# Fourier mixing and GEGLU layers: z^T by VectorE and a round trip through DRAM, layer norm statistics by ScalarE

## The chip, the cores and the metric

The kernel runs on one core of a Trainium2 chip. TensorE (PE) multiplies; PEld is the loading of its stationary operand, which overlaps with it. VectorE (DVE), ScalarE (ACT) and GpSimd (POOL) work on tiles in SBUF, the first two on PSUM as well. SyncE (SP) issues loads from DRAM on one queue, POOL issues most stores on another; both use the core's 16 DMA engines. The metric is the time on the device in microseconds (us), the median of several runs.

## The reference

Four layers over x of 2048 x 512 in fp32: layers 0 and 2 are Fourier mixing, layers 1 and 3 a GEGLU feed-forward, each behind a layer norm without gains and with its input added back.

```python
def _layernorm(x, axis=-1, eps=1e-5):
    m = jnp.mean(x, axis=axis, keepdims=True)
    v = jnp.var(x, axis=axis, keepdims=True)
    return (x - m) / jnp.sqrt(v + eps)
def _A_ref(x, dft_seq_re, dft_seq_im, dft_hid_re, dft_hid_im):
    a = jnp.einsum("bsd,ed->bse", x, dft_hid_re)
    b = jnp.einsum("bsd,ed->bse", x, dft_hid_im)
    y = jnp.einsum("ts,bse->bte", dft_seq_re, a) - jnp.einsum("ts,bse->bte", dft_seq_im, b)
    return y
def _B_ref(x, w_gate, w_up, w_down):
    return (_gelu(x @ w_gate) * (x @ w_up)) @ w_down
x = x + _A_ref(_layernorm(x), ...)
x = x + _B_ref(_layernorm(x), ...)
x = x + _A_ref(_layernorm(x), ...)
x = x + _B_ref(_layernorm(x), ...)
```

The sequence matrices are 2048 x 2048, the hidden ones 512 x 512, w_gate and w_up 512 x 1792, w_down 1792 x 512. They come in as arrays, so the kernel reads them; it assumes nothing of their values.

## The kernel before, in words

*Precision.* Every fp32 operand of a product is split into a high part in fp32r (ACT, L110) and the rest (DVE, L111), and `mm3` (L142 to L146) makes one product out of three matmuls: high by high, high by low, low by high. A matmul takes 128x128 weights and 128x512 moving data.

*Fewer products.* The large products are done by one step of a Strassen-Winograd scheme on 2 x 2 blocks: seven block products instead of eight, whose operands are sums and differences of blocks (names S1 to S4 on the matrix's side, T1 to T4 on the side of the normalized input z). Sums are DVE's (`plus`, L135; `minus`, L132); copies out of PSUM are ACT's (`copied`, L139).

*Tiles.* Everything lies in slots of 128 x 512 fp32 in SBUF (`sb`, 102 of them) and eight PSUM banks (`ps8`). A slot that is freed goes to the end of a list and is taken again in that order, so a load into it waits for its last reader.

*Mixing layers (0 and 2).* `plan` runs over four blocks b of 512 rows of the sequence matrices, and within each over stages (A11, A12, S2, S3, A22 on the sequence side, then three groups of the hidden side). A stage runs over k, the 128-row tiles of z along the sequence, eight to a half. For each k, `take` hands out the next matrix tile `ws` of a list `items`: it loads ahead (four items ahead of the split, which is up to five ahead of the use: RAW = 4, AHEAD = 5) and splits ahead. The contraction is over the sequence, so here z is used as it is, rows on partitions.

*GEGLU layers (1 and 3).* Two halves w of 1024 tokens. Gate and up products are made transposed, features on partitions, so z^T is wanted: `block_steps` (L441) normalizes eight row tiles, and PE turns them with 128x128 transposes against an identity (`turned`, L450 to L457, 16 into four PSUM banks' width for each group of four tiles). From PSUM the blocks are copied, subtracted and split. `up(n)` makes the gate or up product of one pair of feature tiles in seven block products; from n = 6 on, steps of the down product (`down_steps`) are put between them; afterwards the remaining down products run one after the other, part 0 and then part 1, and `x_add` adds the input's rows and stores them (POOL's queue). The split down weights lie in DRAM as `wd`, the split and summed gate and up weights as `wb`; both are made once. `weight_steps` makes `wb` from the raw `wgu`, in layer 1 with the first half's work; `down_weight_steps` makes `wd` during layer 0.

*Layer norm.* `normed` (L368): DVE's bn_stats and bn_aggr, an addition of eps, POOL's power of -1/2, DVE's product for the shift, and ACT's scaling of the row tile (L382).

*The order.* Work that isn't on the path of products stands as closures in a list `queue`; `step` runs the next one after a product. In layers 0 and 2 a step follows each k, in the down products each item, in layer 1's first half each block product. On top of this a scheduler of the framework orders each engine's instructions by times that it reckons itself. The program orders SP's DMAs by eight semaphores in turn.

## Time and profile before

| | |
|---|---|
| median of 3 runs | 1665.11 us (1663.8 to 1665.39) |
| profiled execution | 1666.76 us, its span 1664.9 us |
| PE, PEld | 1650.4 and 1359.2 us busy (99%, 82%) |
| DVE, ACT, POOL | 1190.7, 776.2 and 169.3 us busy (72%, 47%, 10%) |
| DMA | 388.46 MB, 233 GB/s over the span |

Busy time of PE is that of pipelined matmuls whose ends are modelled, so 99% doesn't say that PE is at its peak; the chain of work that ended last tells better what sets the end. In the groups by line a row gives the line, the engine, the operation, output and inputs with their sizes, the count, busy time and mean duration, and the idle time of the engine just before with what ended it. Transposes, copies and splits all run through helpers, so their lines are those of the helpers. Layer 0 lasts to about 440 us, layer 1 to 845, layer 2 to 1210, layer 3 to the end.

### The profile page before, as it was taken

To read this page: it belongs to the slowest core of one execution; us is meant where nothing else is said; L and a number is where in the kernel's file an instruction comes from. 1 tells how busy PE (TensorE), PEld (TensorE's weight loads), DVE (VectorE), ACT (ScalarE), POOL (GpSimd) and SP (SyncE) were. 2 spreads that over 40 slices of the span, in tenths; PEclk is the share of its full clock that TensorE was granted. 3 is DMA by queue.
4 is the path that set the end of the run, shared out by engine and by line. 5 is a ranking of instruction groups with operands and counts; after the bars stand their busy time and mean duration, and the time that the engine had idled before them with its cause. 6 is when DMAs were issued, how large, how long until landed. Compare 5 with 4: busy or idle time off the path is not lost.

```text
span 1664.9 us, 22527 instructions
## 1 busy us (share of the span) xinstructions
PE 1650.4 (99%) x7296; PEld 1359.2 (82%) x7296; DVE 1190.7 (72%) x2132; ACT 776.2 (47%) x1352; POOL 169.3 (10%) x288
## 2 busy tenths in 40 slices
PE   9999999999999999999999999999999999999999
PEld 6877788888788888888888888888888888888887
DVE  8997978687887765655898785857946556656561
ACT  7744434255565543534663333444635443444440
POOL 3212100021422110000210000000100000100000
PEclk9999999999999999999999999999999999999999
DMA  9788886778766876555665766565695559755551
GB/s 361 247 279 329 306 317 227 253 252 291 273 229 215 292 269 233 172 189 198 216 227 182 240 228 228 168 227 188 225 386 184 171 177 321 259 178 175 186 183 51
DMA packets 200726, 388.46 MB, mean 233 GB/s; under 512 B 23840, under 2 KB 27424, under 8 KB 200608
## 3 DMA queue, kind: packets, MB, share of 16 engines
q1 hardware_dynamic: 183168, 329.86, 59.1%
q0 software_dynamic: 17440, 57.16, 9.1%
q8 instruction: 58, 0.95, 0.2%
q14 instruction: 60, 0.49, 0.1%
HBM read 328.73 MB, written 58.20 MB: 232 GB/s over the span
## 4 chain that ended last, share of the span: by engine, by line
PE 93%; DVE 3%; DMA 2%; issue 1%; ACT 1%; SPq 0%; DVEq 0%; ACTq 0%
PE p L144 31%; PE p L145 30%; PE p L146 30%; DMA s<-wgu 2%; DVE s L111 1%; PE p L551 1%; PE p L454 1%; DVE s L135 1%; DMA s<-ws 1%; DVE s L132 1%; DMA s<-x 0%; DVE s L725 0%; DVE s L739 0%; DVE s L723 0%; ACT s L110 0%
## 5 line engine op out<-in xcount | busy, mean ns | idle before, releaser
L145 PE MATMUL p<-s,s 128*128 128x512 f32 x2368 | 921.7, 390 | 1.9 <-DVE s L111 1.9
L146 PE MATMUL p<-s,s 128*128 128x512 f32 x2368 | 908.6, 390 | 0.0
L144 PE MATMUL p<-s,s 128*128 128x512 f32 x2368 | 901.2, 391 | 7.0 <-DVE s L135 3.9
L110 ACT ACTIVATE s<-s 128x512 fp32r<-128x512 f32 (+1 forms) x758 | 438.0, 617 | 467.6 <-DVE s L132 98.6
L111 DVE TENSOR_TENSOR s<-s,s 128x512 fp32r<-128x512 f32 (+1 forms) x758 | 490.2, 679 | 87.1 <-ACT s L110 64.3
L144 PEld LDWEIGHTS p<-s,s 128*128 128x128 f32 x2368 | 445.0, 188 | 102.9 <-DVE s L135 5.0
L145 PEld LDWEIGHTS p<-s,s 128*128 128x128 f32 x2368 | 445.4, 188 | 95.0 <-DVE s L111 3.1
L146 PEld LDWEIGHTS p<-s,s 128*128 128x128 f32 x2368 | 445.2, 188 | 93.7 <-DVE s L111 0.7
L135 DVE TENSOR_TENSOR s<-s,p 128x512 f32<-128x512 f32 x316 | 213.0, 685 | 188.9 <-PE p L146 140.6
L139 ACT ACTIVATE s<-p 128x512 f32<-128x512 f32 x248 | 145.2, 593 | 187.4 <-PE p L146 171.4
L132 DVE TENSOR_TENSOR s<-s,s 128x512 f32<-128x512 f32 (+1 forms) x290 | 172.4, 608 | 23.4 <-DMA s<-ws 15.4
L722 ACT ACTIVATE s<-s 128x512 f32<-128x512 f32 x112 | 70.4, 630 | 91.7 <-DVE s L135 90.9
L725 DVE SCALAR_TENSOR_TENSOR s<-s,s 128x512 f32<-128x512 f32 x112 | 76.8, 690 | 38.2 <-ACT s L724 37.6
L378 POOL TENSOR_TENSOR rstd<-rstd,power 128x1 f32<-128x1 f32 x64 | 50.8, 803 | 506.7 <-DVE rstd L377 500.8
L723 DVE SCALAR_TENSOR_TENSOR s<-s,s 128x512 f32<-128x512 f32 x112 | 77.0, 690 | 33.5 <-ACT s L722 31.3
L724 ACT ACTIVATE s<-s 128x512 f32<-128x512 f32 x112 | 69.5, 627 | 25.0 <-DVE s L723 24.4
L135 DVE TENSOR_TENSOR s<-s,s 128x512 f32<-128x512 f32 (+1 forms) x78 | 50.1, 645 | 38.5 <-DMA s<-ws 22.1
L169 POOL DMA_DIRECT2D x<-s x48 | 26.1, 543 | 443.8 <-DVE s L135 440.8
L382 ACT ACTIVATE s<-s,shift,rstd 128x512 f32<-128x512 f32 x64 | 50.4, 811 | 36.5 <-DVE shift L380 32.1
L739 DVE SCALAR_TENSOR_TENSOR s<-s,s 128x512 f32<-128x512 f32 x84 | 58.0, 690 | 1.6
L197 POOL DMA_DIRECT2D wb<-s x84 | 45.2, 540 | 121.6 <-ACT s L110 85.1
L373 DVE BATCH_NORM_STATS2 st<-s 128x6 f32<-128x512 f32 x64 | 42.7, 689 | 19.8 <-DMA s<-x 19.8
(32 smaller groups left out, 254.6 us busy)
## 6 DMA issues: line engine op xcount, KB each, us to landing
s<-ws SPq DMA_DIRECT2D x432, 256.0 KB, 4.0
s<-wb SPq DMA_DIRECT2D x294, 256.0 KB, 4.1
s<-wd SPq DMA_DIRECT2D x224, 256.0 KB, 4.3
s<-x SPq DMA_DIRECT2D x126, 256.0 KB, 4.1
s<-wh SPq DMA_DIRECT2D x120, 256.0 KB, 4.8
wb<-s POOLq DMA_DIRECT2D x98, 256.0 KB, 3.5
x<-s POOLq DMA_DIRECT2D x48, 256.0 KB, 4.1
wd<-s POOLq DMA_DIRECT2D x28, 256.0 KB, 4.9
```

The costliest lines, as they stand in the source:

```text
L110: nc.scalar.activation(hi, src, AF.Copy)
L111: nc.vector.tensor_tensor(lo, src, f32(hi), op=ALU.subtract)
L132: nc.vector.tensor_tensor(out, a, b, op=ALU.subtract)
L135: nc.vector.tensor_tensor(out, a, b, op=ALU.add)
L139: nc.scalar.activation(v, src, AF.Copy)
L144: nc.tensor.matmul(ps, ah, bh, start=start, stop=False, skip_group_check=True)
L145: nc.tensor.matmul(ps, ah, bl, start=False, stop=False, skip_group_check=True)
L146: nc.tensor.matmul(ps, al, bh, start=False, stop=stop, skip_group_check=True)
L722: nc.scalar.activation(t, g, AF.Square)
L723: nc.vector.scalar_tensor_tensor(t, t, 1.0 / GELU_C, g, op0=ALU.add, op1=ALU.mult)
L724: nc.scalar.activation(t, t, AF.Tanh, scale=GELU_A * GELU_C)
L725: nc.vector.scalar_tensor_tensor(t, t, 1.0, g, op0=ALU.add, op1=ALU.mult)
```

## The change: what it does

- *z^T.* Each normalized 128x512 tile is turned by DVE in 32x32 blocks into one wide tile of 128 x 2048 (one buffer); when four tiles are in it, POOL stores it (1 MB) to DRAM, and SP reads z^T back, each 128x512 tile by four DMAs of 32 partitions with runs of 128 fp32 (512 bytes). The transposes on PE and the copies out of PSUM are gone.
- *Row order.* The tokens of a 512-token group come out in another order: column tile j holds the rows 32j to 32j + 31 of each of the four row tiles. So x lies in DRAM in groups of 512 rows, and the GEGLU layers load and store it with four runs of 32 rows to a tile (`rows(..., mixed=True)`). The last four tiles of a GEGLU layer's output stay in SBUF for the next mixing layer, in that order, and `seq_tile` reads the sequence matrix's rows for k of 12 and above in four runs of 32 rows to match (layer 2 alone).
- *Statistics.* In layers 1 to 3 ACT makes the sum (Copy with an accumulator), the mean, the sum of squared deviations (Square with bias and an accumulator); POOL divides by 512, adds eps and takes the power; ACT makes the shift. Layer 0 keeps DVE's statistics. Half of layer 2's are made ahead in layer 1's second half (`terms_ahead`), from rows loaded for it.
- *Weights.* `down_weight_steps` is gone: the down weights are loaded raw, split and stored at their first use in layer 1's first half (`make_down_first`). The loads of `weight_steps` are a step of their own, issued earlier than the sums and splits.
- *Order.* The norms of layers 1 and 3 stand in the queue of block 2 (of 0 to 3) of the mixing layer ahead, instead of the last stage but one; `step` follows each block product of the up phase; items that come split from DRAM are read ahead by two beyond the use and two beyond the split (NEAR = 2). There are 98 slots instead of 102, and a pool of twelve for the early statistics.

```diff
+NEAR = 2
 EARLY = 2
 SKEW = 2
-NSLOT = 102
+NSLOT = 98
...
-    og = out.rearrange("(n p) d -> n p d", p=P)
-    xs = {(0, i): xg[i] for i in range(NS)}
+    xg = x_in.rearrange("(g r) d -> g r d", r=TB)
+    og = out.rearrange("(g r) d -> g r d", r=TB)
+    xs = {(0, g): xg[g] for g in range(NB)}
     for layer in range(1, 4):
-        for i in range(NS):
-            xs[layer, i] = dram.tile([P, D], F32, name=f"x{layer}_{i}")
-    xs.update({(4, i): og[i] for i in range(NS)})
+        for g in range(NB):
+            xs[layer, g] = dram.tile([TB, D], F32, name=f"x{layer}_{g}")
...
     fresh = {}
-    def x_load(layer, i):
+    def rows(layer, i, mixed=False):
+        g, n = divmod(i, NT)
+        if mixed:
+            return xs[layer, g].rearrange("(n j t) d -> j n t d", n=NT, t=32)[n]
+        return xs[layer, g][n * P:(n + 1) * P]
+    def x_load(layer, i, mixed=False):
         t = sb.get()
-        nc.sync.dma_start(t, xs[layer, i])
+        nc.sync.dma_start(t, rows(layer, i, mixed))
...
-    def x_add(layer, i, t, ps, keep=False, engine=nc.gpsimd):
+    def x_add(layer, i, t, ps, mixed=False, keep=False, engine=nc.gpsimd):
         plus(t, t, ps)
         ps8.put(ps)
-        engine.dma_start(xs[layer + 1, i], t)
+        engine.dma_start(rows(layer + 1, i, mixed), t)
...
     def split_next():
         n = stream["split"]
         while stream["loaded"] <= min(n + RAW, len(items) - 1):
+            if stream["loaded"] > n + NEAR and items[stream["loaded"]][2] is whole:
+                break
             load_next()
         parts[n] = items[n][2](*raws.pop(n))
...
             need = items[stream["split"]][3]
             if need and need not in cs and stream["split"] > n:
                 break
+            if items[stream["split"]][2] is whole and stream["split"] > n + NEAR:
+                break
             split_next()
...
+    def whole(*parts):
+        return parts
+    def make_down_first(f):
+        def run(v):
+            p = plain(v)
+            kept(wds[f], p)
+            return p
+        return run
...
+    def seq_tile(layer, n, k):
+        if layer and k >= NS - NT:
+            return ws[(n + 1) * NS - NT:(n + 1) * NS, (k % NT) * 32:(k % NT + 1) * 32]
+        return ws[n * NS + k]
...
-        for _ in range(NB // 2):
-            items.extend((F32R, halves(wds[f]), lambda *w: w, None) for _ in range(2) for f in range(NF))
+        for w in range(NB // 2):
+            for part in range(2):
+                for f in range(NF):
+                    if layer == w == part == 0:
+                        items.append((F32, (wdn[f],), make_down_first(f), None))
+                    else:
+                        items.append((F32R, halves(wds[f]), whole, None))
...
+    known = {}
+    def row_of(layer, i):
+        x = fresh.pop(i, None)
+        return x_load(layer, i) if x is None else x
+    def norm_terms(layer, i, x, junk):
+        pool = spool if layer == 0 else kpool
+        rstd = pool.tile([P, 1], F32, name="rstd")
+        shift = pool.tile([P, 1], F32, name="shift")
+        if layer == 0:
+            st = spool.tile([P, 6], F32, name="st")
+            nc.vector.bn_stats(st, x)
+            mv = spool.tile([P, 2], F32, name="mv")
+            nc.vector.bn_aggr(mv, st)
+            nc.vector.tensor_scalar_add(rstd, mv[:, 1:2], EPS)
+            nc.gpsimd.tensor_tensor(rstd, rstd, power, op=ALU.pow)
+            nc.vector.scalar_tensor_tensor(shift, mv[:, 0:1], -1.0, rstd, op0=ALU.mult, op1=ALU.mult)
+        else:
+            total = spool.tile([P, 1], F32, name="total")
+            mean = spool.tile([P, 1], F32, name="mean")
+            nc.scalar.activation(junk, x, AF.Copy, accum_out=total)
+            nc.scalar.activation(mean, total, AF.Copy, scale=-1.0 / D)
+            nc.scalar.activation(junk, x, AF.Square, bias=mean, accum_out=rstd)
+            nc.gpsimd.tensor_scalar(rstd, rstd, 1.0 / D, EPS, op0=ALU.mult, op1=ALU.add)
+            nc.gpsimd.tensor_tensor(rstd, rstd, power, op=ALU.pow)
+            nc.scalar.activation(shift, mean, AF.Copy, scale=rstd)
+        return rstd, shift
+    def terms_ahead(layer, i):
+        x, junk = x_load(layer, i), sb.get()
+        known[layer, i] = norm_terms(layer, i, x, junk)
+        sb.put(x, junk)
     def normed(layer, i):
-        x = fresh.pop(i, None)
-        if x is None:
-            x = x_load(layer, i)
-        st = spool.tile([P, 6], F32, name="st")
-        nc.vector.bn_stats(st, x)
-        mv = spool.tile([P, 2], F32, name="mv")
-        nc.vector.bn_aggr(mv, st)
-        rstd = spool.tile([P, 1], F32, name="rstd")
-        nc.vector.tensor_scalar_add(rstd, mv[:, 1:2], EPS)
-        nc.gpsimd.tensor_tensor(rstd, rstd, power, op=ALU.pow)
-        shift = spool.tile([P, 1], F32, name="shift")
-        nc.vector.scalar_tensor_tensor(shift, mv[:, 0:1], -1.0, rstd, op0=ALU.mult, op1=ALU.mult)
+        x = row_of(layer, i)
         z = sb.get()
...
     def block_steps(layer, w):
-        z, t = {}, {}
+        zt, t, wide = {}, {}, {}
+        turned = [dram.tile([P, NT * D], F32, name=f"t{layer}_{w}_{part}") for part in range(2)]
         def norm(i):
             def run():
-                z[i] = normed(layer, w * 2 * NT + i)
+                z = normed(layer, w * 2 * NT + i)
+                part, n = divmod(i, NT)
+                if n == 0:
+                    wide[part] = tpool.tile([P, NT * D], F32, name="wide")
+                to = wide[part].rearrange("p (b n t) -> p b n t", n=NT, t=32)
+                nc.vector.transpose(to[:, :, n], z.rearrange("p (b t) -> p b t", t=32))
+                sb.put(z)
+                if n == NT - 1:
+                    nc.gpsimd.dma_start(turned[part], wide.pop(part))
             return run
...
-            if c == ND - 1:
-                sb.put(*(z.pop(part * NT + i) for i in range(NT)))
-            return ps
+        def fetch(c):
+            def run():
+                for part in range(2):
+                    v = zt[c, part] = sb.get()
+                    for i in range(P // 32):
+                        cols = turned[part][:, (c * 4 + i) * P:(c * 4 + i + 1) * P]
+                        to = v[i * 32:(i + 1) * 32]
+                        nc.sync.dma_start(
+                            to.rearrange("p (j t) -> p j t", t=P), cols.rearrange("(j p) t -> p j t", p=32)
+                        )
+            return run
...
         def first(c):
             def run():
-                ps = turned(c, 0)
-                t[f"B{1 + c // 2}1", c % 2] = copied(ps)
-                blocks[f"B{1 + c // 2}1", c % 2] = split_slot(ps)
-                ps8.put(ps)
+                v = t[f"B{1 + c // 2}1", c % 2] = zt.pop((c, 0))
+                blocks[f"B{1 + c // 2}1", c % 2] = split_slot(v)
             return run
         def second(c):
             def run():
-                ps = turned(c, 1)
+                v = zt.pop((c, 1))
                 if c < 2:
-                    t["B12", c] = copied(ps)
-                    t["T1", c] = difference(ps, t["B11", c])
+                    t["B12", c] = v
+                    t["T1", c] = difference(v, t["B11", c])
                     sb.put(t.pop(("B11", c)))
                 else:
                     c0 = c - 2
-                    t["T2", c0] = difference(ps, t["T1", c0])
-                    t["T3", c0] = difference(ps, t["B12", c0])
+                    t["T2", c0] = difference(v, t["T1", c0])
+                    t["T3", c0] = difference(v, t["B12", c0])
                     sb.put(t.pop(("B12", c0)))
-                    blocks["B22", c0] = split_slot(ps)
-                ps8.put(ps)
+                    blocks["B22", c0] = split_slot(v)
+                    sb.put(v)
             return run
...
-        two = [norm(i) for i in range(NT, 2 * NT)] + [second(c) for c in range(ND)]
+        one = [norm(i) for i in range(2 * NT)]
+        two = [fetch(c) for c in range(ND)] + [first(c) for c in range(ND)] + [second(c) for c in range(ND)]
         two += [fourth(c) for c in range(2)]
         two += [divide(name, c) for name in ("T2", "T3", "T1", "T4") for c in range(2)]
-        return one + two
+        return one, two
...
             sides[b] = side
+            if b == NB - 2:
+                norms, others = block_steps(layer + 1, 0)
+                queue.extend([run for norm in norms[:NT] for run in (norm, None)])
+                rest.extend((norms[NT:], others))
             if last and layer == 0:
-                queue.extend(weight_steps(0))
+                opening_weights.update((n, weight_steps(n)) for n in range(2))
+                queue.extend([opening_weights[0][0], None, opening_weights[1][0], None, *opening_weights[0][1]])
             for second, k in skewed():
                 if second:
...
             if last:
-                queue.extend(block_steps(layer + 1, 0))
+                queue.extend(rest[1])
                 if layer == 0:
-                    queue.extend(weight_steps(1))
+                    queue.extend(opening_weights[1][1])
+            if b == NB - 2:
+                queue.extend([run for norm in rest[0] for run in (norm, None)])
             for second, k in skewed():
                 if second:
...
-        return [load, store]
+        return load, [sums] + [divide(i) for i in range(len(pieces))]
     def weight_load(n):
         tiles = [sb.get(F32R) for _ in range(7)]
@@ -759,14 +823,16 @@
                 yield
             sb.put(*hs, *v)
-        making = layer == 1 and w == 0
+        making = {}
+        if layer == 1 and w == 0:
+            making.update((n, weight_steps(n)) for n in range(2, NF))
+            making[2][0]()
         chain, side, c11, u, w4 = {}, {}, {}, {}, {}
         def product(n, ps, an, bn, start, stop):
-            if making:
-                step()
+            step()
             hi, lo = wparts[n][an]
             for c in range(2):
                 cut = slice(c * P, (c + 1) * P)
...
         def up(n, down):
+            if n + 3 in making:
+                making[n + 3][0]()
+            if n + 2 in making:
+                queue.extend(making[n + 2][1])
             product(n, chain[n], "S2", "T2", False, True)
             u[n] = copied(chain[n])
             next(down, None)
...
             sb.put(*wparts.pop(n)["tiles"])
-            if making and n + 3 < NF:
-                queue.extend(weight_steps(n + 3))
-            elif not making and n + 2 < NF:
+            if not making and n + 2 < NF:
                 weight_load(n + 2)
         def down(f, part):
...
-                x_add(layer, (w * 2 + 1) * NT + i, xrows.pop(0), acc[1][i], engine=nc.sync)
+                x_add(layer, (w * 2 + 1) * NT + i, xrows.pop(0), acc[1][i], True, engine=nc.sync)
...
         load_rows(0)
-        if before_mix:
+        if w == 0:
+            queue.extend(run for part in block_steps(layer, 1) for run in part)
+        elif before_mix:
             queue.extend((lambda k=k: first_rows(layer + 1, k)) for k in range(NK))
+            for k in range(NT):
+                queue.append(lambda k=k: second_rows(layer + 1, k))
+                queue.append(lambda k=k: combine(k))
+            queue.extend((lambda k=k: combine_late(k)) for k in range(NT))
         for f in range(NF - LAG, NF):
             down(f, 0)
         add_rows(0)
         if w == 0:
             weight_load(0)
             weight_load(1)
-            queue.extend(block_steps(layer, 1))
-        elif before_mix:
-            for k in range(NT):
-                queue.append(lambda k=k: second_rows(layer + 1, k))
-                queue.append(lambda k=k: combine(k))
...
         queue += [lambda k=k: combine_late(k), None]
-    for run in [run for f in range(NF) for run in down_weight_steps(f)]:
-        queue += [run, None, None]
     for layer in range(4):
```

37 lines of the change are left out of this document (12 added, 25 removed).

## The prediction

> **What bounds the kernel now.** I read the page's busy table first, then the chain that ended last, then the groups by line, then windows over single stages, then the DMA view.
>
> ```profile
> span 1664.9 us, 22527 instructions
> PE 1650.4 (99%) x7296; PEld 1359.2 (82%) x7296; DVE 1190.7 (72%) x2132; ACT 776.2 (47%) x1352; POOL 169.3 (10%) x288
> PE 93%; DVE 3%; DMA 2%; issue 1%; ACT 1%; SPq 0%; DVEq 0%; ACTq 0%
> ```
>
> TensorE is the bound: 93% of the chain lies on it. What it issues counts, then, unless a change makes it wait. From the chain in order of time and from the windows (columns: stretch, PE busy and count, PEld, DVE, ACT, POOL, clock, DMA share, GB/s):
>
> ```profile
> 889.51 0.68 PE p L144 x3
> 1195.54 1.75 PE p L454 x16
> ...
> 430.00:446.00 16.00, 13.12 (x55) 10.06 (x54) 10.32 (x21) 8.68 (x16) 4.83 (x9) 0.98 0.76 266
> 845.00:1210.00 365.00, 365.00 (x1627) 302.26 (x1626) 284.33 (x498) 169.62 (x294) 18.24 (x30) 1.00 0.65 214
> 1210.00:1560.00 350.00, 350.00 (x1561) 290.05 (x1561) 203.78 (x335) 151.09 (x261) 12.08 (x20) 1.00 0.67 228
> ```
>
> A product matmul (L144) takes 0.68/3 = 0.227 us of the chain, a transpose (L454) 1.75/16 = 0.109. From 845 to 1560 us PE is busy without a gap. Around the start of layer 1 it is not: 55 matmuls are 55 x 0.227 = 12.5 us of the 16, so 3.5 us are lost there. The stage 845 to 1210 is layer 2; its DMA share of 0.65 will matter.
>
> ```profile
> L454 PE MATMUL p<-ident,s 128*128 128x128 f32 x128 | 17.0, 272 | 0.0
> L139 ACT ACTIVATE s<-p 128x512 f32<-128x512 f32 x248 | 145.2, 593 | 187.4 <-PE p L146 171.4 <-PE p L454 10.7 <-DVE s L725 2.2
> L110 ACT ACTIVATE s<-s 128x512 fp32r<-128x512 f32 x728 | 427.3, 626 | 459.2 <-PE p L146 95.0 <-DVE s L132 90.4 <-PE p L145 65.7
> L111 DVE TENSOR_TENSOR s<-s,s 128x512 fp32r<-128x512 f32 x728 | 478.8, 690 | 85.8 <-ACT s L110 63.0 <-PE p L145 6.7 <-PE p L146 5.5
> L373 DVE BATCH_NORM_STATS2 st<-s 128x6 f32<-128x512 f32 x64 | 42.7, 689 | 19.8 <-DMA s<-x 19.8
> L375 DVE BATCH_NORM_AGGREGATE mv<-st 128x2 f32<-128x6 f32 x64 | 10.3, 176 | 0.1
> L377 DVE TENSOR_SCALAR rstd<-mv 128x1 f32<-128x1 f32 x64 | 8.2, 151 | 0.4
> L380 DVE SCALAR_TENSOR_TENSOR shift<-mv,rstd 128x1 f32<-128x1 f32 x64 | 9.9, 158 | 11.6 <-POOL rstd L378 11.1
> L378 POOL TENSOR_TENSOR rstd<-rstd,power 128x1 f32<-128x1 f32 x64 | 50.8, 803 | 506.7 <-DVE rstd L377 500.8 <-ACT s L110 2.7 <-DVE shift L380 2.2
> L80 ACT ACTIVATE warm<-warm 128x1 f32<-128x1 f32 x1 | 0.2, 204 | 0.0
> ```
>
> And the DMA view (share of 16 engines; issue to landing in us), with the waits of 845 to 1210 us:
>
> ```profile
> DMA packets 200726, 388.46 MB, mean 233 GB/s; under 512 B 23840, under 2 KB 27424, under 8 KB 200608
> q1 hardware_dynamic: 183168, 329.86, 59.1%
> s<-ws SPq DMA_DIRECT2D x432, 256.0 KB, 4.0
> s<-wd SPq DMA_DIRECT2D x224, 256.0 KB, 4.3
> ...
> s<-wgu SPq DMA_DIRECT2D x28, 128.0 KB, 3.4
> ...
> out<-s SPq DMA_DIRECT2D x4, 256.0 KB, 2.0
> ```
>
> ```profile
> ACT s L110 <- DMA s<-ws: 31.7, 16, 4.5
> ...
> DVE s L135 <- DMA s<-ws: 13.3, 7, 3.0
> DVE s L132 <- DMA s<-ws: 12.6, 14, 2.4
> ```
>
> In layer 2, ACT and DVE already wait 57.6 us for the sequence matrix's tiles, which does not reach PE because tiles are split ahead of their use.
>
> **The change part by part.** *Transposes off PE.* 128 x 0.109 = 14.0 us leave the chain. The group's mean of 272 ns is a pipelined duration, not a spacing. The Trainium skill (TensorE: Matmul & The Clock Gate, Part 4: PE-mode transpose) gives a transpose in a kernel about 275 ns; by that 35.2 us would go, 21.2 more than by the chain. The duration agrees with it, the spacing of 0.109 us does not, and it is the spacing that PE pays.
>
> *Copies and statistics.* Off ACT: 24 copies out of PSUM, 24 x 0.593 = 14.2 us. Off DVE: the statistics of 48 row tiles, 48 x (689+176+151+158 ns) = 56.4 us. Onto DVE: 32 transposes of 128x512. No row shows one; ends 0.69 us (any fp32 pass, L111) and twice that for its scattered write. I take 0.69, 22.1 us: as many elements per partition. Onto ACT: 48 x (2 x 0.626 + 2 x 0.204) = 79.7 us; onto POOL 48 more small operations, 48 x 0.803 = 38.5. An accumulating pass may take longer than 0.626; the dear end is L382's 811 ns, 0.2 us more. Net DVE falls by 34 us, ACT rises to 842, about 51%. Busy time is covered on both, but the order is not free: the shift on ACT now stands behind ACT, POOL, POOL, and whatever is queued on ACT behind it (splits that PE needs, and loads into the slots that these free) waits 2 x 0.803 = 1.6 us per tile. In layer 2's third block four tiles stand close together there. Ends 0 and 4 x 1.6 = 6.4 us; I take 3.
>
> *The way through DRAM.* Eight stores of 1 MB on POOL's queue, 128 loads of 64 KB on SP's. A 64-KB load is bounded by 2.0 us (the fastest 256-KB row) and 3.4 (the 128-KB row). SP's DMAs use eight semaphores in turn, so at most eight fly: 32 loads take at most 32/8 x 3.4 = 13.6 us, the store before them no more than four times a 256-KB landing of 4.3, 17 us. In the changed program's order, the transposed half that is latest against its use is layer 3's last: from what its last transpose needs to the first matmul that reads it stand 122 matmuls, 27.7 us. The store at half its dear end plus the loads fit, at both dear ends 3 us are missing. I take 0.
>
> *Weights.* The down weights' 14 loads of 256 KB, splits and stores leave layer 0 for their first use in layer 1, where 28 loads back fall away: 14 x (0.626 ACT, 0.690 DVE) moves, beside PE. The gate weights' loads are issued a step earlier, which meets the 3.5 us lost at 430 to 446; ends 0 and 3.5, and I take 3.5, as the loads then have a stage instead of their landing. *The shorter read-ahead* (NEAR) leaves the down weights four items of 12 matmuls, 4 x 2.7 = 10.9 us, over a landing of 4.3: nothing.
>
> *The order of rows.* The transposes leave a 512-token block in an order of 4 x 32 rows. So 32 loads of x, 32 stores of x and, in layer 2, 64 loads of the sequence matrix (all for k of 12 and above) have in DRAM an outer count of 4, not 128. A 256-KB load costs 0.262/329.86 x 0.591 x 1664.9 = 0.78 us on each of 16 engines. No row shows a load with an outer count under 128. Ends: 0.78 us as now, or, if rows are dealt by the outer count, four engines carry it alone: 3.13 us on them. I take the second: the 23840 small packets are 16 for each of the 1490 DMAs of the table (17 rows, of which the first and the last stand above), so each is closed by 16 engines with equal shares of 128 rows, and four blocks cannot be shared equally by more than four.
>
> The Trainium skill (DMA: Bandwidth & Descriptors, Rules for kernel authors) has this rule: an outermost size under 16 confines a DMA to that many engines. No trace here can show it yet.
>
> Layer 2, then: 0.65 x 365 = 237 us busy per engine now. Less 64 x 0.78 = 50, plus 64 x 3.13 = 200, plus z^T's 4 MB (two stores, eight tiles read) 12: 399 us on four engines in a stage of 365. Every 128-row load also needs those four, so all loads queue: 34 us short. Were everything a tenth cheaper, 359 us, nothing would be short. It is uneven too: in the new order, at the layer's start, six of seven loads that follow each other are such, 6 x 3.13 + 0.78 = 19.6 us, plus 2.0 landing and 1.3 for the split, and the seventh is used 64 matmuls, 14.5 us, after the first may go: 8 us late. The read-ahead of 40 to 100 matmuls (9 to 23 us, 4.0 of it the landing now) smooths some 10 us once. Layer 2 loses 34 - 10 = 24 us; ends 0 and 34 + 8 = 42. ACT's 3 us hide in it. Between the halves of layer 1, where the four x loads, 14 gate weights and z^T's 32 loads meet, 4 more (ends 0 and 14).
>
> The sum: -14.0 - 3.5 + 24 + 4 = +10.5 on the profiled execution's 1666.76 us (span 1664.9 and 1.9 around it): 1677.3. That execution stood 1.65 above the median, so 1675.6; I say 1676.
>
> **The rivals.**
> *All 16 engines carry the 4 x 32 loads.* For it: nothing in the profile shows them confined, and DMA has a third of layer 2 free. Then layer 2 keeps 3 us of ACT's waits: 1665.1 - 14.0 - 3.5 + 3 = 1651, faster; it decides once a 4 x 32 load lands in about the 4.0 us of the others. 30 in 100.
> *Four engines, but the read-ahead covers most.* DMA's price is at its low end, layer 2 loses 10, the halves nothing: 1665.1 - 17.5 + 10 = 1658 to 1662. Against it: the 57.6 us of waits for these tiles today. 12 in 100, 5 faster and 7 within 0.2%.
> *The way through DRAM is late.* The first of a half's loads waits for the store at the head of SP's in-order queue, and the down weights behind it wait too: at the store's dear end 17 us, against a read-ahead of 10.9, so 6.1 at each of four places, and the 3 us missing at the tight one: 1665.1 - 17.5 + 24.4 + 3 = 1675, slower. It decides once the queue is held for over 10.9 us. Against it: a 256-KB store lands in about the time of a load, so 17 us would need four of them one after the other. 3 in 100.
>
> **How the numbers follow.** The forecast has 55 in 100, its own range 1668 to 1700. A difference under 0.2% (3.3 us) can't be told from none here. Slower: 55 + 3 = 58; same 7; faster 30 + 5 = 35. The range must reach the first rival: 1648 to 1699, leaving out some 7 below and 8 above.
>
> **What would show it.** Right: no L454 and PE without waits at block changes; in layer 2 ACT and DVE wait for ws far beyond 57.6 us, ws landings well above 4.0, PE gaps in 845 to 1210 of some 24 us, and fewer than 16 small packets for each of these DMAs. At 430 to 446 no PE gap. Wrong: 4 x 32 loads that land like the rest, or PE full in layer 2; then the first rival holds and the time is near 1651. Much over 1700 would mean that the queue of four engines reaches layers 1 and 3 as well.

## The result, and the profile after

The changed kernel takes 1855.53 us (median; 1848.99 to 1857.9) beside 1665.25 us for the kernel before on the same chip: ratio 1.1135, 95% interval 1.1104 to 1.1167. The forecast was 1676 us, range 1648 to 1699. The direction was right, the size was not: 190 us instead of 11. The profiled execution of the changed kernel took 1857.9 us, 2.4 above its median.

From the page of the changed kernel: the span, the busy engines, TensorE's granted clock in 40 slices (tenths), the chain that ended last by engine, and the packets.

```profile
span 1856.1 us, 22573 instructions
PE 1693.9 (91%) x7168; PEld 1372.4 (74%) x7168; DVE 1168.8 (63%) x1972; ACT 839.2 (45%) x1616; POOL 193.9 (10%) x344
PEclk9999999999999889999788999989979999989999
PE 51%; issue 23%; DMA 16%; DVE 5%; ACT 3%; SPq 1%; POOL 1%; DVEq 0%; ACTq 0%; POOLq 0%
DMA packets 221607, 400.03 MB, mean 216 GB/s; under 512 B 29872, under 2 KB 49840, under 8 KB 220464
```

PE has 128 instructions fewer and is busy 43.5 us longer (1693.9 against 1650.4), at a clock that now falls in the middle of the span. The chain, 93% PE before, is 51% PE, and 16% DMA stands in it.

Windows over the stages, each from its first product matmul to the next stage's (columns as in the prediction's windows: stretch, PE busy and count, PEld, DVE, ACT, POOL, clock, DMA share, GB/s). The stages are layer 0, layer 1's two halves, layer 2, layer 3's two halves. First the kernel before, then the changed one:

```profile
7.50:414.80 407.30, 401.43 (x1745) 325.48 (x1745) 350.47 (x652) 208.76 (x364) 67.47 (x105) 1.00 0.82 287
414.80:633.70 218.90, 215.84 (x958) 177.51 (x957) 165.28 (x312) 113.53 (x206) 54.52 (x102) 0.99 0.74 259
633.70:843.10 209.40, 209.40 (x925) 173.40 (x924) 138.52 (x260) 103.11 (x178) 11.88 (x20) 1.00 0.60 195
843.10:1238.60 395.50, 395.50 (x1761) 327.50 (x1760) 299.20 (x522) 176.81 (x307) 20.21 (x34) 1.00 0.68 227
1238.60:1451.70 213.10, 213.10 (x958) 176.70 (x957) 127.45 (x217) 94.12 (x161) 9.92 (x17) 1.00 0.67 226
1451.70:1660.90 209.20, 209.20 (x925) 173.21 (x923) 106.67 (x163) 77.61 (x133) 3.57 (x7) 1.00 0.49 163
```

```profile
7.80:417.70 409.90, 402.06 (x1713) 324.84 (x1713) 344.63 (x620) 213.75 (x398) 63.78 (x99) 0.98 0.80 271
417.70:639.00 221.30, 212.09 (x925) 174.03 (x924) 153.25 (x275) 122.23 (x246) 67.32 (x126) 0.98 0.75 256
639.00:867.00 228.00, 215.28 (x926) 176.50 (x925) 129.44 (x211) 120.79 (x251) 16.22 (x32) 0.97 0.66 208
867.00:1410.00 543.00, 432.14 (x1730) 342.95 (x1729) 308.38 (x503) 198.34 (x383) 26.71 (x48) 0.88 0.57 175
1410.00:1621.60 211.60, 209.78 (x926) 173.10 (x924) 109.01 (x169) 96.46 (x190) 12.53 (x25) 1.00 0.66 215
1621.60:1846.80 225.20, 215.86 (x923) 174.93 (x924) 120.84 (x187) 85.29 (x146) 5.57 (x8) 0.97 0.59 184
```

So layer 0 ends at 415 us, layer 1 at 843 and layer 2 at 1239, and not at 440, 845 and 1210 as said ahead of the prediction. Layer 2 alone lost 147.5 us of the 191.2 between the spans, and the second halves of layers 1 and 3 another 18.6 and 16.0; 5.3 us more lie behind the last matmul (1856.1 - 1846.8 against 1664.9 - 1660.9), where the last stores are. Note the DMA share of layer 2: it fell from 0.68 to 0.57. The stage became longer than its transfers; the sixteen engines as a whole were never the limit. The waits of layer 2 (867 to 1410) say for whom it waited:

```profile
ACT s L113 <- DMA s<-ws: 112.2, 31, 9.7
...
DVE s L138 <- DMA s<-ws: 51.3, 15, 7.4
...
DVE s L135 <- DMA s<-ws: 38.8, 18, 4.0
```

202 us for the tiles of the sequence matrix, against 57.6 before, and now they reach PE, which waits 35.4 us there for ACT's splits and 34.4 for DVE's.

### The profile page after: what moved, and what is told of

It reads as the page before. It is cut to its first block, busy times and chain, and to the rows that moved or that the text cites. A ratio compares the mean times of both kernels' runs of the same rounds, so it can differ in the third digit from the quotient of the medians.

```text
span 1856.1 us, 22573 instructions
## 1 busy us (share of the span) xinstructions
PE 1693.9 (91%) x7168; PEld 1372.4 (74%) x7168; DVE 1168.8 (63%) x1972; ACT 839.2 (45%) x1616; POOL 193.9 (10%) x344
## 2 busy tenths in 40 slices
DMA packets 221607, 400.03 MB, mean 216 GB/s; under 512 B 29872, under 2 KB 49840, under 8 KB 220464
## 4 chain that ended last, share of the span: by engine, by line
PE 51%; issue 23%; DMA 16%; DVE 5%; ACT 3%; SPq 1%; POOL 1%; DVEq 0%; ACTq 0%; POOLq 0%
PE p L148 17%; PE p L147 17%; PE p L149 17%; DMA s<-ws 6%; DMA s<-x 4%; DVE s L114 2%; DVE s L135 2%; DMA x<-s 1%; DMA s<-wb 1%; DMA s<-wh 1%; ACT s L113 1%; DVE s L138 1%; DMA s<-wd 1%; PE p L624 1%; DMA s<-wgu 1%
## 5 line engine op out<-in xcount | busy, mean ns | idle before, releaser
L147 PE MATMUL p<-s,s 128*128 128x512 f32 x2368 | 921.8, 400 | 110.2 <-ACT s L113 48.2
L148 PE MATMUL p<-s,s 128*128 128x512 f32 x2368 | 941.3, 398 | 39.3 <-DVE s L114 38.1
L149 PE MATMUL p<-s,s 128*128 128x512 f32 x2368 | 922.4, 396 | 2.3 <-DVE s L114 2.3
L113 ACT ACTIVATE s<-s 128x512 fp32r<-128x512 f32 (+1 forms) x782 | 452.6, 616 | 612.8 <-DMA s<-ws 130.7
L114 DVE TENSOR_TENSOR s<-s,s 128x512 fp32r<-128x512 f32 (+1 forms) x782 | 504.3, 675 | 242.6 <-ACT s L113 188.4
L147 PEld LDWEIGHTS p<-s,s 128*128 128x128 f32 x2368 | 455.3, 193 | 219.8 <-ACT s L113 72.1
L148 PEld LDWEIGHTS p<-s,s 128*128 128x128 f32 x2368 | 455.4, 192 | 148.5 <-DVE s L114 51.5
L149 PEld LDWEIGHTS p<-s,s 128*128 128x128 f32 x2368 | 453.9, 192 | 98.7 <-DVE s L114 3.4
L135 DVE TENSOR_TENSOR s<-s,s 128x512 f32<-128x512 f32 (+1 forms) x314 | 185.9, 609 | 81.2 <-DMA s<-ws 45.9
L142 ACT ACTIVATE s<-p 128x512 f32<-128x512 f32 x224 | 130.5, 591 | 146.9 <-PE p L149 141.2
L786 ACT ACTIVATE s<-s 128x512 f32<-128x512 f32 x112 | 70.3, 629 | 75.2 <-DVE s L138 74.4
L138 DVE TENSOR_TENSOR s<-s,s 128x512 f32<-128x512 f32 (+1 forms) x78 | 49.6, 640 | 82.9 <-DMA s<-ws 67.5
L788 ACT ACTIVATE s<-s 128x512 f32<-128x512 f32 x112 | 70.0, 626 | 24.4 <-DVE s L787 23.8
L429 POOL TENSOR_SCALAR rstd<-rstd 128x1 f32<-128x1 f32 x48 | 13.6, 282 | 426.9 <-ACT s L428 389.2
L426 ACT ACTIVATE s<-s 128x512 f32<-128x512 f32 x48 | 29.9, 623 | 59.4 <-DMA s<-x 39.3
```

What stands on the lines that cost most here:

```text
L113: nc.scalar.activation(hi, src, AF.Copy)
L114: nc.vector.tensor_tensor(lo, src, f32(hi), op=ALU.subtract)
L135: nc.vector.tensor_tensor(out, a, b, op=ALU.subtract)
L138: nc.vector.tensor_tensor(out, a, b, op=ALU.add)
L142: nc.scalar.activation(v, src, AF.Copy)
L147: nc.tensor.matmul(ps, ah, bh, start=start, stop=False, skip_group_check=True)
```

## The experiments

Stages in us, each kernel's profiled execution, from the trace by the first product matmul of each stage (L1 and L3 have two halves, a and b). Three of these executions lie far from their kernel's median: a_nat's 7.9 us under it, b_98's 4.5 and b_ws8's 4.3 us over it. The names are those of the expectations below.

```
                 L0    L1a    L1b     L2    L3a    L3b    median us
before         407.3  218.9  209.4  395.5  213.1  209.2    1665
after          409.9  221.3  227.9  542.9  211.7  225.2    1855.5
a_ws16         407.6  225.4  227.4  413.9  211.0  225.0    1729.0
a_x16          409.2  213.5  215.7  528.9  209.4  217.1    1807.6
a_all16        409.0  211.7  217.4  413.5  209.4  217.9    1691.9
a_nat          407.1  209.4  216.4  399.9  209.4  209.2    1672.8
a_nat1         415.2  212.0  210.3  403.1  209.4  209.2    1671.2
a_nat1_dve     415.2  212.4  209.4  401.7  209.4  209.2    1669.2
a_nat1w        414.0  209.4  210.3  402.1  209.4  209.2    1666.6
a_nat1w_dve    412.1  209.4  209.5  397.9  209.4  209.2    1662.0
a_nat1_ws4     412.0  211.5  210.3  512.9  209.4  209.2    1780.6
b_ws4          405.8  218.7  209.4  486.4  213.1  209.2    1755.9
b_ws4_98       412.7  218.6  209.4  486.1  213.1  209.2    1763.5
b_ws8          406.6  219.5  209.4  424.0  213.1  209.2    1690.6
b_spread4      406.4  218.3  209.4  463.1  213.1  209.2    1734.1
b_98           411.3  221.7  209.4  400.8  213.2  209.2    1674.7
b_act          406.2  214.2  209.4  409.1  214.1  209.2    1677.3
```

**Which of the transfers with an outer count of four?** The 64 ws loads of layer 2 and the 64 x transfers were each split into four transfers of 32 rows, alone and together.

```diff
+            if len(a.shape) == 3:                # a_ws16: a ws tile out of four
+                for i in range(NT):
+                    stream["last"] = nc.sync.dma_start(to[i * 32:(i + 1) * 32], a[i])
...
+        if mixed:                                # a_x16: loads; stores likewise
+            for j in range(NT):
+                nc.sync.dma_start(t[j * 32:(j + 1) * 32], rows(layer, i, mixed)[j])
```

> The changed kernel with one edit: each of the 64 ws loads of layer 2 that takes 32 rows from each of four tiles is issued as four loads of 32 rows (outer count 32). The x loads and stores of layers 1 and 3 keep their outer count of four. Theory 1 (the ws loads with outer count four make layer 2's loss): layer 2 goes from 542.9 us to about 400 and the time from 1855 to about 1710. Theory 2 (the loss in layer 2 comes from the statistics on ScalarE, the 98 slots or the look-ahead of the new order): layer 2 stays within 20 us of 543 and the time stays above 1830. The second halves of layers 1 and 3 stay at 228 and 225 us under both.

> The changed kernel with the 32 x loads and 32 x stores of layers 1 and 3 each issued as four transfers of 32 rows; the ws loads of layer 2 keep outer count four. Theory 3 (x transfers on four engines hold up the second halves): the second halves of layers 1 and 3 go from 228 and 225 us back to about 210 each, and the time from 1855 to about 1821. Its rival (the way of z^T through DRAM is late there whatever the x transfers do): they stay at 225 to 228 and the time stays at 1850 to 1860. Layer 2 stays at about 543 us under both.

> Both edits together: no transfer with an outer count of four is left, all else is the changed kernel. Theories 1 and 3: about 1655 to 1680, with layer 2 at 395 to 405 us and both second halves at about 210. If the statistics, the slots or the way through DRAM carry the loss: above 1800.

Measured: 1729.0 (ratio to before 1.0389, 1.0369 to 1.0408), 1807.6 (1.0856, 1.0840 to 1.0872) and 1691.9 us (1.0177, 1.0137 to 1.0217). The ws loads cost 126.5 us of the 190, 129 of them in layer 2 (542.9 to 413.9). The x transfers cost 48: 14 in layer 2, 12 and 8 in the second halves, 8 in layer 1's first, 2 in layer 3's first, 4 behind the last matmul. Both together do not bring layer 2 back to 395.5 or the second halves back to 209; 18 and 8 us stay, and a_all16 missed the 1655 to 1680 expected of it. The statistics, the slots or the order could explain at most that.

**Are the loads enough by themselves, and how do they cost?** The kernel before was given nothing but these loads; then with eight engines, with 98 buffers, and spread over every fourth tile. In all four the tiles' rows stand in another order than z's, so layer 2 makes other numbers out of the same work.

```diff
+        if layer and k >= NS - NT:
+            return ws[(n + 1) * NS - NT:(n + 1) * NS, (k % NT) * 32:(k % NT + 1) * 32]       # b_ws4
+            return ws[n * NS + NS // 2:(n + 1) * NS, (k % NT) * 16:(k % NT + 1) * 16]        # b_ws8
+        if layer and k % NT == NT - 1:
+            return ws[n * NS + k - NT + 1:n * NS + k + 1, 96:]                               # b_spread4
...
-NSLOT = 102
+NSLOT = 98                                                                               # b_ws4_98, b_98
```

> The kernel before with one edit: the 64 ws loads of layer 2 for row tiles 12 to 15 take 32 rows from each of four tiles (outer count four), as in the changed kernel. The rows of these tiles then stand in another order than z, so that layer 2's result is not the reference's; the work is the same. Theory 1: layer 2 goes from 395.5 to about 530 us and the time from 1665 to about 1800. Theory 2: at most 30 us more, under 1695. The forecast's own ledger (throughput of four engines) would give 24 us more, about 1690.

> The kernel before with the 64 ws loads of layer 2 for row tiles 12 to 15 taken as 16 rows from each of eight tiles (outer count eight instead of four). Layer 2's result is not the reference's; the work is the same. Where the four engines' own queues fill up in each burst of eight such loads (S3 with A22, nominal 32.7 us: with four engines 8 x 3.5 and about 18 x 0.8 us make 42 us of their time), eight engines need 8 x 1.75 + 18 x 0.8 = 28 us, less than the burst lasts: layer 2 at 395 to 410 us instead of 486, the time 1665 to 1680. Where each such load is simply late in proportion to its engines, about half of the 91 us stays: 1705 to 1715.

> The kernel before with the 64 ws loads of outer count four in layer 2 (486.4 us there, against 528.9 us for the same loads in the changed kernel's own order) and 98 buffers instead of 102. If the four buffers that the wide tile takes are what makes the same loads dearer in the changed kernel: layer 2 goes from 486 to 515 to 530 us, the time from 1756 to 1785 to 1800. If it is the new order of the norms and the limit on the read-ahead: layer 2 stays within 8 us of 486 and the time within 10 us of 1756.

> The kernel before in which the ws loads of outer count four are spread over layer 2: those of every fourth row tile (3, 7, 11 and 15) instead of the last four (12 to 15); 52 loads instead of 64. Layer 2's result is not the reference's; the work is the same. If each such load costs by itself, or by the mean load of four engines over the layer, the loss shrinks only with the count, 91 x 52/64 = 74 us: layer 2 at 465 to 475 and the time at 1735 to 1742. If it is the bunching (four in a row need 4 x 3.5 us of the four engines where PE uses a tile in 1.36 us; one in four needs 3.5 + 3 x 0.8 = 5.9 us for 5.4 us of PE's work in A11, A12 and A22, and only S2, which loads two or three tiles per step, stays short, by some 30 us in all), layer 2 comes to 415 to 440 and the time to 1685 to 1710.

b_ws4 took 1755.9 us (1.0544, 1.0526 to 1.0561): the loads by themselves cost the kernel before 91 us, more than four times the ledger's 24 and less than the 129 of the changed kernel. Its packets, with b_ws8's and b_spread4's (whole execution), and the windows over layer 2 of b_ws4 and b_ws8:

```profile
DMA packets 199958, 388.46 MB, mean 221 GB/s; under 512 B 23072, under 2 KB 26656, under 8 KB 199840
841.50:1327.90 486.40, 418.50 (x1762) 337.08 (x1761) 300.80 (x522) 175.75 (x307) 20.17 (x34) 0.93 0.57 183
```

```profile
DMA packets 200214, 388.46 MB, mean 229 GB/s; under 512 B 23328, under 2 KB 26912, under 8 KB 200096
842.80:1266.80 424.00, 404.34 (x1762) 332.33 (x1761) 300.30 (x523) 176.28 (x307) 20.51 (x34) 0.98 0.66 209
```

```profile
DMA packets 200102, 388.46 MB, mean 224 GB/s; under 512 B 23216, under 2 KB 26800, under 8 KB 199984
```

The small packets settle the first step. Before there were 23840; with 64 loads of four there are 768 = 64 x 12 fewer, with 64 of eight 512 = 64 x 8 fewer, with 52 of four 624 = 52 x 12 fewer. Each such load is closed by exactly as many engines as its outer count, and so carried by as many. That is what the Trainium skill (DMA: Bandwidth & Descriptors, Rules for kernel authors) says; the trace agrees. The changed kernel's own trace has it too. Of its 29872 small packets 24496 are of 4 bytes, 16 for each of 1606 DMAs less 12 for each of 100, and SyncE has 100 transfers with an outer count of four: 64 ws loads, 32 x loads and 4 stores. The other 5376 are of 8 bytes, 192 for each of POOL's 28 mixed stores, so for POOL's queue this count doesn't tell the engines; but layer 1's 16 x stores land there 9.6 us after their issue (median), in the kernel before 4.6.

Where the rows lie in DRAM is not the reason for the loss: a_ws16 reads the same rows by four transfers on all engines.

The size is another matter. From issue to landing, taken from the trace's DMA and semaphore records for 256-KB loads in layer 2 (least and median, us), with the loss of the layer:

```
                  loads of 4 or 8     128-row loads      loss of layer 2, per such load
before                  -              2.45   4.1         -
b_ws8  (64 of 8)    4.16   5.6         2.47   5.1        28.5    0.45
b_spread4 (52 of 4) 5.11   7.7         2.44   5.4        67.6    1.30
b_ws4  (64 of 4)    5.37   8.2         2.46   5.4        90.9    1.42
after  (64 of 4)    5.54   8.9         2.48   5.4       147.4      -
```

I had expected bunching to be the reason: four such loads in a row against one in four. b_spread4 (1.0419, 1.0393 to 1.0445) refutes that. Expected were 415 to 440 us for layer 2, or 465 to 475 if each load costs by itself; it was 463.1, and 1.30 us per load is close to 1.42. b_ws8 (1.0148, 1.0121 to 1.0175) lay between both of its expectations; by the medians its loss is 25 us, 0.39 per load. 98 buffers (b_ws4_98, 1.0597, 1.0578 to 1.0617) change nothing in layer 2; its 7.6 us over b_ws4 stand in layer 0.

Where in layer 2 the time goes can be read by its stages (nominal, then measured, us, summed over the four blocks):

```
            nominal   before   b_ws4   b_spread4   b_ws8   after
A12            43.5     43.5    58.4       49.4     45.0    71.6
S2             87.1     87.2   112.3      114.7     92.1   132.7
S3             87.1     89.2   133.0      115.9    105.3   151.2
A22            43.5     45.0    52.1       52.5     51.0    49.7
```

A11 and the hidden side stay at their nominal times, but for 7 us in the changed kernel's A11. S3 lost most under b_ws4 (44 us), then S2 (25). While S3 runs (32 to 35 us in b_ws4), SyncE issues 15 to 23 loads of ws and wh, for it and already for A22, four to six of them of four engines; in the other stages it issues at most 12 of these. What in this is the four engines' own time and what the in-order reuse of buffers that land late, these runs do not separate.

**Why more in the changed kernel's order?** a_nat1_ws4 is the changed kernel without any other transfer of four and with one fetch per chunk of z^T (see below), and with these 64 loads.

> The changed kernel with natural rows and one fetch of 128 rows per chunk in all halves, to which only the 64 ws loads of outer count four are given back (layer 2's result is then not the reference's; the work is the same). Natural rows alone gave layer 2 in 399.9 us; the kernel before lost 91 us to these loads, the changed kernel with all else on sixteen engines 115 more (528.9 against 413.5). If the 32 fetches of 32 rows in the last S3 of layer 2 are part of what makes the loads dearer in the changed kernel: that stage goes from 42.5 us to 30 to 34 and layer 2 comes to 510 to 520. If the fetches do not matter: that stage stays at 41 to 43 and layer 2 at 524 to 532.

Measured 1780.6 us (1.0701, 1.0682 to 1.0719), layer 2 in 512.9, its last S3 33.1 instead of a_x16's 42.5, as expected if the 32 fetches of z^T on the same queue cost this stage 9 us (the two kernels differ in the x transfers too). The loads then cost 512.9 - 403.1 = 110 us, still 19 more than in the kernel before. Five of these 19 stand in the third S2 (26.0 us in a_nat1, 34.6 with the loads; 21.8 and 25.4 in the kernel before), where the changed kernel loads x for norms; that these loads do it was not tried, and the rest stays open.

**Natural rows, and the way of z^T.** In a_nat the order of rows is put right where h is split, so that all of x and ws are 128-row transfers again. In a_nat1 the store of z^T, in four parts, puts the 512-byte runs in place, and each chunk is one fetch of 128 rows. a_nat1w does that in the second halves alone. The suffix _dve keeps the statistics on VectorE in all layers.

```diff
-                h[f, part] = split_slot(t)
+                h[f, part] = split_slot(t.rearrange("p (j n t) -> p n j t", n=NT, t=32), True)      # a_nat
...
-                    nc.gpsimd.dma_start(turned[part], wide.pop(part))                           # a_nat1
+                    to, v = turned[part].rearrange("(b a) (j u) -> j a b u", a=32, u=P), wide.pop(part)
+                    for j in range(NT):
+                        nc.gpsimd.dma_start(to[j], v[j * 32:(j + 1) * 32].rearrange("a (b u) -> a b u", u=P))
...
+                    nc.sync.dma_start(v, turned[part][c * P:(c + 1) * P])
...
-        if layer == 0:                                                                           # _dve
+        if True:
             st = spool.tile([P, 6], F32, name="st")
```

> The changed kernel, with the row order put right inside the kernel: the split of h into its two parts reads its 512 columns in the order (n, j, t), so that the down product's row tiles hold natural rows; x loads, x stores and layer 2's ws loads are plain 128-row transfers, as many as before the change. If what is left of layer 2's loss in the kernel without outer counts of four (413.5 against 395.5 us) is the time that SyncE needs to issue four loads per tile (4 x 0.47 us against 1.36 us per tile of ws), layer 2 comes to 395 to 400 us and the time to 1660 to 1672; the second halves, with 12 issues fewer for each set of four x loads, to 210 to 215. If it is the statistics on ScalarE, the order or the 98 slots: layer 2 at 408 to 415 and the time at 1678 to 1690.

> The kernel with natural rows, and the way of z^T turned round: the store, by four transfers of 256 KB instead of one of 1 MB, puts its runs of 512 bytes where they belong, and each chunk is fetched by one load of 128 rows instead of four of 32: 8 fetches for 32 per half. If the second halves' last delay is SyncE's queue (32 fetches x 0.47 us = 15 us in a row, just ahead of their use), they come to 209 to 211 us, and the time is 6 to 14 us less than that of the kernel with natural rows alone, 1650 to 1660. If the delay is the norms or the store (the first fetch waits for the last of the store), the time stays within 3 us of that kernel's.

> The same kernel with the statistics of all layers by VectorE (bn_stats, as in the first layer), the order and all else unchanged. If the statistics on ScalarE cost nothing or gain nothing on the path: within 4 us of the kernel beside it. If they relieve VectorE (1167 us busy with them on ScalarE): slower by 5 to 20 us. If the longer chain on ScalarE holds up the start of layer 2: faster by 5 to 15.

> The changed kernel with natural rows (the split of h reads its columns in the order n, j, t), and with the way of z^T turned round (four stores of 256 KB, one fetch of 128 rows per chunk) in the second halves of layers 1 and 3 alone; the first halves keep the changed kernel's way. If the second half of layer 1 waits for the 32 fetches and the first layer for the four stores: layer 0 at 407 us (not 415), the second half of layer 1 at 210 (not 216), and the time 5 to 8 us under both kernels with natural rows, 1660 to 1667. If the first layer's 8 us came from another order of its loads that any edit can bring about: no better than 1668.

> The same with the statistics of all layers on VectorE. Covered statistics: within 4 us of the kernel beside it. If the chain on ScalarE holds up layer 2's start: 2 to 6 us less.

a_nat: 1672.8 us (1.0040, 1.0024 to 1.0056). Its profiled execution, at 1664.9, was the fastest of its runs, so its stages in the table are some 8 us better than its median. Layer 2 comes to 399.9, in a_nat1 to 403.1: of the 18 us left by a_all16, 10 to 14 went with the split loads, as expected for SyncE's time to issue four of them per tile. The same queue bears on the second halves. In a_all16, SyncE's timeline from 1461 us and the wait at that place (1465 to 1480), where layer 3's second half begins (1468.5):

```profile
1461.41 0.38 SPq L789 DMA_DIRECT2D s<-wb  x1
1461.89 16.57 SPq L542 DMA_DIRECT2D s<-t  x32
1478.57 1.79 SPq L789 DMA_DIRECT2D s<-wb  x4
```

```profile
ACT s L113 <- DMA s<-t: 21.3, 5, 18.1
```

32 fetches take SyncE 16.57 us, 0.52 each, and ACT stands 18.1 us for one of them. With 8 fetches instead, layer 1's second half goes from 216.4 to 210.3 (a_nat1, a_nat1w; the store of z^T changed with them, and no run has one without the other). Layer 3's was at 209.2 in a_nat already, with all its 32 fetches: they begin at 1429.9 us there, 20 us ahead of the half, while in a_all16 the 16 split x loads hold SyncE for 11 us just before them. The medians hardly moved at first, 1671.2 (1.0034, 1.0021 to 1.0047), within the 3 us that a_nat1's expectation had for another cause of the delay. Layer 0 stands 8 us longer in the table than a_nat's, but a_nat's profiled execution was its fastest, so where the gain went is not shown. a_nat1w, 1666.6 (1.0013, 1.0002 to 1.0024), has 414.0 there too: the four stores in the first halves are not what does it. With the statistics on VectorE, a_nat1_dve took 1669.2 (1.0022, 1.0008 to 1.0035) and a_nat1w_dve 1662.0 (0.9986, 0.9976 to 0.9996): 2 and 5 us less, of which the 2 are within the intervals. The last one is the only kernel here whose interval lies below the kernel before, and by less than the 0.2% that count as a difference.

**The statistics alone, and the buffers alone.**

> The kernel before with the statistics of layers 1 to 3 by ScalarE's accumulator and nothing else changed (transposes stay on TensorE). If the statistics are covered, as the forecast has it: 1663 to 1669 us. If the longer chain (two passes and two reads of the accumulator on ScalarE, 623 + 187 + 710 + 187 ns, against bn_stats on VectorE) comes on the path where a layer starts: 1670 to 1685.

> The kernel before with 98 buffers instead of 102, nothing else. If the 7 us that the first layer lost with 98 buffers (412.7 against 405.8 us, both with the loads of outer count four in layer 2) come from the four buffers: layer 0 at 411 to 415 us and the time at 1669 to 1674. If they came from another order of the loads there: 1663 to 1668.

b_act (the six lines of `norm_terms` for layers 1 to 3 in `normed`): 1677.3 us (1.0072, 1.0059 to 1.0085), 12 us slower. Layer 1's first half became 5 us shorter and layer 2 14 longer, over half of it where layer 2 starts (its first A12 18.3 us for 10.9). There the norms are followed by their use; the changed kernel makes the terms of eight rows ahead and pays 2 to 5. b_98: 1674.7 us (1.0060, 1.0047 to 1.0072). Four buffers fewer cost the kernel before 10 us, in layer 0, layer 1's first half and layer 2 (this execution was its slowest, 4.5 us over the median, so the shares are rough):

```profile
7.70:419.00 411.30, 403.64 (x1744) 327.20 (x1745) 350.32 (x652) 208.20 (x364) 68.55 (x105) 0.99 0.82 282
419.00:640.80 221.80, 217.62 (x958) 178.32 (x957) 164.16 (x310) 115.29 (x206) 53.68 (x100) 0.98 0.72 254
640.80:850.20 209.40, 209.40 (x925) 173.39 (x924) 138.87 (x261) 102.66 (x177) 14.28 (x20) 1.00 0.61 197
850.20:1251.00 400.80, 397.20 (x1762) 327.01 (x1761) 300.59 (x523) 179.46 (x308) 19.64 (x34) 1.00 0.67 222
```

So I tried to give them back: the wide tile out of four of 102 buffers, held only while in use, with four transposes of 128 columns per z (a_slot, and a_slot_dve with the statistics on VectorE).

```diff
-                    wide[part] = tpool.tile([P, NT * D], F32, name="wide")
+                    wide[part] = [sb.get() for _ in range(ND)]
```

> The changed kernel with natural rows and one fetch per chunk in the second halves, in which the wide tile is four of 102 buffers, held only while the four transposes and the store need them, instead of four buffers' space held for good; each z is turned by four transposes of 128 columns instead of one of 512 (DVE 96 instructions more). If the four buffers are what costs the first layer 5 to 8 us: layer 0 from 414 to 406 to 409 us and the time from 1667 to 1658 to 1662. If not, or if the 96 instructions and the 16 stores of 64 KB come on the path: 1665 to 1672.

> The same with the statistics on VectorE in all layers. Going by the pair without the buffers (1662 against 1667), 4 to 5 us less than the kernel beside it: 1654 to 1658 if the buffers count, 1660 to 1666 if not.

Both are misses: 1686.3 us (1.0125, 1.0112 to 1.0138) and 1681.3 (1.0103, 1.0088 to 1.0119). Layer 1's first half is 220.7 and 218.0 instead of 209.4, and layer 2's third S2, where the four buffers are taken beside the read-ahead (that this is the reason was not tried), 32.4 and 27.4 us instead of 26.4 and 23.2. Layer 0 did not gain what the four buffers would be worth either (411.0 and 415.3). What the changed kernels' layer 0 loses against 407 us is therefore not settled, though b_98, in its slowest execution, loses 4 us there by the buffers alone.

## Why the prediction was wrong

**Transposes off PE, -14.0: right.** Where nothing else holds PE the whole of it shows. Layer 3's first half has 32 matmul records fewer (958, then 926) and goes from 213.1 to 209.4 in a_x16, a_all16 and every a_nat kernel: 3.7 us, and four such places would make 14.8.

**Weights, -3.5: right.** From 430 to 446 us PE has 72 matmuls instead of 55 and no gap, in the changed kernel; in its layer 1 the first gap of over 0.3 us stands 170 us behind the layer's start, before the change 26 us:

```profile
430.00:446.00 16.00, 16.00 (x72) 13.25 (x71) 15.50 (x29) 12.19 (x23) 6.78 (x14) 1.00 0.88 319
```

**Copies and statistics, 3: right in size, for the changed order; ScalarE's durations were not.** The transpose took 698 ns (taken 690), POOL's two operations 282 and 676 (taken 803 each). ScalarE's part came to 2.18 us per tile instead of 1.66: two passes of 623 and 710, after each a read of the accumulator of 187, which the forecast had no term for, the mean 190 and the shift 284.

```profile
L515 DVE STREAM_TRANSPOSE wide<-s 128x512 f32<-128x512 f32 x32 | 21.8, 698 | 13.2 <-DMA t<-wide 9.9 <-ACT s L443 3.2
L428 ACT ACTIVATE s<-s,mean 128x512 f32<-128x512 f32 x48 | 34.1, 710 | 0.2
L426 ACT ACTIVATION_READ_ACCUMULATOR s<-s 128x1 f32 x48 | 9.0, 187 | 0.0
L431 ACT ACTIVATE shift<-mean,rstd 128x1 f32<-128x1 f32 x48 | 13.4, 284 | 6.5 <-POOL rstd L430 6.5
L430 POOL TENSOR_TENSOR rstd<-rstd,power 128x1 f32<-128x1 f32 x48 | 32.4, 676 | 3.5
```

On VectorE the kernel takes 2 to 5 us less (a_nat1_dve, a_nat1w_dve); in the second pair 3 of them stand in layer 2's third S2 (26.4, then 23.2), the block that the forecast named. But b_act shows 12 us without the terms made ahead, over half of layer 2's part in its first A12: what counts is the chain's length where its result is used at once.

**The way through DRAM, 0: wrong by 6 us in layer 1's second half.** The forecast bounded 32 loads by eight semaphores, 13.6 us, over a cover of 27.7. What it left out is that SyncE needs 0.52 us to issue each (16.57 us), and that x loads and weights stand in the same queue ahead of them. In layer 3's second half the fetches cost nothing by themselves (209.2 us in a_nat). The third rival's condition, SP's queue held for over 10.9 us, came true, and the forecast gave it 3 in 100; but that rival had the queue wait for the store, and here the issuing held it.

**The slots, not in the sum: a missing term.** 98 buffers instead of 102 cost the kernel before 10 us. Of the diff's two new constants the forecast priced the read-ahead's and left this one out.

**Four engines carry a 4 x 32 transfer: right. The price, +24 (ends 0 and 42): the step that failed.** The time of such a load on its four engines was not far off: in bunches they land 3.5 us apart (median in b_ws4; taken 3.13). The ledger was. It set the four engines' work, summed over the layer, against the layer's time, found 34 us short, and took it that nothing more is lost. (Its window of 365 us was not all of layer 2; over the 395.5 the same sum gives 0.68 x 395.5 - 50 + 200 + 12 = 431 us, 35 short.) By the same reckoning from b_ws4's and b_ws8's own windows no engine was full: 0.57 x 486.4 us is the mean of sixteen; 64 loads of 128 packets (2 KB, 0.1 us each in the trace) lie on four of them, 51.2 us of that mean, so the four were busy for some 0.57 x 486.4 - 51.2 + 204.8 = 431 of 486 us, and with eight 0.66 x 424 - 51.2 + 102.4 = 331 of 424. With eight the ledger predicts no loss, and 28.5 us were lost. This kernel, which reads up to nine tiles ahead, loses time before the engines' sum is full, and in the same runs each such load, and the 128-row loads beside them, land later (median 4.1 before, 8.2 and 5.4 in b_ws4). The loss goes roughly with the number of such loads, 1.3 to 1.4 us for each on four engines and 0.4 on eight. The bunching I put in the ledger's place was refuted by b_spread4. A model that gives these two numbers I do not have.

In the changed kernel the same term is 115 to 129 us, by the way the x transfers are sent: to the kernel before's 91 come the z^T fetches in the same queue (some 9, by a_nat1_ws4) and others that no run names.

**Halves of layer 1, +4 (ends 0 and 14): past its upper end.** Layer 1's second half lost 18.5 us, and layer 3's, for which there was no term, 16.0: 12 and 8 to x transfers with an outer count of four, 6 of the rest of layer 1's went with the single fetches (a_nat1); layer 3's rest is gone with natural rows (a_nat). "Much over 1700 would mean that the queue of four engines reaches layers 1 and 3 as well" holds for a smaller part: x transfers cost 34 of the 190 us outside layer 2, but layer 2 alone went far past the bound set for it.

**The rivals.** 1651 with all engines carrying was excluded by the packets. a_nat, which has plain transfers, shows what that rival left out: 1672.8 rather than 1651. Buffers (10 by b_98) and the queue of fetches (6) are some 16 of these 22 us; the rest no run names. That the read-ahead covers most, the second rival, is excluded by b_ws4's 91 us.

## What to carry to other kernels

An access pattern whose outermost count is small cost more here than its share of the engines: look at how late such a load lands against the read-ahead, not at a sum over the stage alone, and at the count of small packets to see how many engines a transfer of SyncE's really has. The cure was to take the new order up inside the kernel, in a pass that was made anyway (the split of h), not in the transfers; splitting each into four left 10 to 14 us of layer 2's loss at the issuing queue, at half a microsecond for each. A change of a buffer count in a diff is a term of the sum, and a queue's issue time another.

## What the runs showed of the hardware

*The clock makes a stall dearer.* PE's own matmuls became slower behind most long stops. PE's timeline in the changed kernel around one (columns: start, duration, what):

```profile
1002.14 0.39 PE L149 MATMUL p<-s,s 128*128 128x512 f32 x1
1016.85 0.80 PE L147 MATMUL p<-s,s 128*128 128x512 f32 x1 [14.32 <-DVE s L138]
1017.44 0.63 PE L148 MATMUL p<-s,s 128*128 128x512 f32 x1
1017.87 0.63 PE L149 MATMUL p<-s,s 128*128 128x512 f32 x1
...
1020.35 0.39 PE L148 MATMUL p<-s,s 128*128 128x512 f32 x1
1020.58 0.40 PE L149 MATMUL p<-s,s 128*128 128x512 f32 x1
```

After 14.3 us without work the starts are 0.425 us apart for 3.5 us, then 0.227 again. Of the 151 us that layer 2 took over its nominal 391.7, 116 are 29 gaps of over 0.6 us from start to start and 34 are starts 0.24 to 0.6 us apart, 121 of them at about 0.425. The granted clock in that stage's window is 0.88, in b_ws4's 0.93, before 1.00. The Trainium skill (TensorE: Matmul & The Clock Gate, Part 1) gives 426.7 ns for a matmul of 512 columns at half clock, and half clock after at least one idle window of about 3.4 us, whose phase is free of the kernel's. The trace agrees with the first, and its records of the granted clock stand at 0.5 for 3.413 us or a multiple of it in this stage. As a bound on the stop the second doesn't hold here: 2.6 us from start to start (at 1294.0) are already followed by six such matmuls, while 3.4 us (at 1052.6) and two stops of 2.0 us (at 1177.7, and at 1116.3 in b_ws4) are followed by none.

*The queue of issues.* 64-KB loads cost SyncE 0.52 us each in a row, and the 256-KB loads behind them 0.45 (four in 1.79 us, in the timeline above): it is the number of transfers that fills this queue.
